# Attention and MLP on one core: the decoding buffers get a pool of their own, two weight sums move into the second token group, and the products get new orders

## The chip, the cores and the metric

One core of one Trainium2 chip runs the whole program. The metric is the device time of one launch in microseconds (us). Inputs lie in the device's memory at the start and the output must lie there at the end. Before the change three runs took 1042.72, 1043.13 and 1045.06 us; the median is 1043.13 us.

## The reference

Sigmoid attention (8 batches, 12 heads, 448 tokens, head size 64) feeds a two-layer MLP with a gated activation. The MLP weights arrive as 64-bit floats.

```python
scores = scale * np.matmul(q, k.transpose(0, 1, 3, 2)) - np.log(S)
attn = 1.0 / (1.0 + np.exp(-scores))
x = np.matmul(attn, v)            # then 3584 tokens x 768
h = x @ w_in                      # 768 x 2048
g = h * (1.0 / (1.0 + np.exp(-1.702 * h)))
out = g @ w_out                   # 2048 x 768
```

## The kernel before

**Stages.** The attention stage runs 48 pairs of heads, two pairs to a unit of 10.3 us, and stores its result by blocks of 512 tokens in device memory (tensor xd). Beside it the 16 pieces of the two weight matrices are decoded from 64-bit words (`decode`, L515): DVE and ACT build exponent and sign in buffers `raw64` and `e`, three DVE instructions build the number, and the result is kept on the chip (the 8 pieces of the first matrix) and stored in device memory (tensor f, one store of 768 KB for each of the 16 pieces).

**The MLP** is a fast matrix multiplication scheme: each of the two matrix products is done as 26 smaller products of sums of blocks. Tokens go in two groups: group 1 has 3 blocks of 512 tokens, group 2 has 4. Group 1 needs 20 of the 26 products of either layer, group 2 all 26, so 92 products in all. One product is 36 matmuls of 128x128 by 128x512 in fp32r (each operand is split in a rounded part and a rest, and three of the four cross terms are taken). For a product, DVE and ACT make the sum of weight blocks (`W_SUMS`: sums 8 to 25 are made from leaves 0 to 7), the sum of token blocks, a rounded copy (a cast, on ACT or DVE) and the rest (a subtraction on DVE) of both, and afterwards add the product into accumulators. In this text a product is named by its layer (0 or 1) and its number (0 to 25).

**Group 1 makes the weight sums**, splits them and saves the split pair in device memory (tensor c); group 2 fetches the saved pairs (`fetched`, L913). The six products that group 1 leaves out (numbers 3, 6, 8, 10, 12 and 17) have the sums 13, 25, 18 and 10 and the leaves 7 and 6. Their four sums are made in group 1 too and stored unsplit (`keep`, L847), and group 2 fetches them unsplit and splits them in place, as it does with leaves. All weight pairs go through a ring of two buffers (`wsplit`): a fetch for product n can only begin when product n-2 has ended. For layer 1, one half of the sums is made ahead during attention (`sums_ahead`, L855).

**SBUF.** All MLP operands lie in slots of an arena. Arena 0 (62 KB per partition) is there from the start; 48 KB of it are taken by the decoded pieces of the first matrix. Arena 1 (104 KB) and the second buffer of the `wsplit` ring lie in the memory of the attention pool `att`, which holds the decoding buffers too (`raw64` 24 KB, `e` 12 KB). They can be written when the last attention transfer has read its buffer.

**The order of the work** is made by a planner at build time (`Plan.run`, L113). It simulates PE, ACT, DVE, the SP queue and the DMA engines with estimated costs, and at each step emits the task that can begin first, ties going to the task whose product is earliest. `HORIZON` (L33) is how many PE tasks ahead of PE a slot may be taken; `KEEP`, `URGENT` and `SPARE` hold back room; `BACKLOG` and `PRESSING` hold back transfers while the modelled DMA backlog is over `BACKLOG` us, unless their product is within `PRESSING` tasks; `GIVE` says how long ACT may be busy for a cast to be still given to it; `RANKED` ranks the decoding among the attention pairs; `ISSUE`, `LANDING` and `PER_KB` are the modelled costs of a transfer. A layer 0 product is four PE tasks, a layer 1 product three. The last entry of each group in `GROUPS` is the order of its products. All transfers are issued by the SP queue, in the planned order.

## Time and profile before

| what | value |
|---|---|
| median of 3 runs | 1043.13 us |
| the profiled execution, its own time | 1042.31 us |
| its span, first to last instruction | 1040.2 us |
| mean granted TensorE clock | 0.993 |
| PE busy | 1012.3 us |
| DVE busy | 900.4 us |
| ACT busy | 631.4 us |
| DMA, both directions | 234.41 MB |

The time of a run is 2.1 us above the span of its profile; the profiled execution is 0.8 us below the median. The attention stage ends at 253.84 us on PE, and the 92 products follow.

### The profile page before, as it was taken

Reading aid. Unit: us, or ns where it says so; the run is one execution under the profiler, and the core shown is the slowest. Engines: PE = TensorE matmul, PEld = TensorE weight load, DVE = VectorE, ACT = ScalarE, POOL = GpSimd, SP = SyncE. Lnnn points to the kernel's source line nnn. Section 1 sums busy time; section 2 is a strip of 40 time slices with the busy share of each in tenths; the row PEclk is TensorE's granted clock in tenths of the full one; section 3 lists DMA queues with packets and bytes.
Section 4 is the critical chain, followed back from the end, with each engine's and each line's share of the span. In section 5 each row is a group of like instructions: output and inputs, shape, how many; then the busy total and the mean of one; then the engine's idle time right before and its main releaser. Section 6 shows DMA issues by size and latency. Waiting matters only on the chain.

```text
span 1040.2 us, 12860 instructions
## 1 busy us (share of the span) xinstructions
PE 1012.3 (97%) x5156; PEld 754.6 (73%) x5156; DVE 900.4 (87%) x628; ACT 631.4 (61%) x496; POOL 0.2 (0%) x4
## 2 busy tenths in 40 slices
PE   9999999999798999889999999999999999999998
PEld 5545454545686888778888777888888877888886
DVE  5999998994998988999989885786898989988876
ACT  6988998885466356676454424365676755553542
POOL 0000000000000000000000000000000000000000
PEclk9999999999899999999999999999999999999999
DMA  9999999996742544444565967544434534343487
GB/s 357 380 373 386 378 414 401 398 390 232 287 159 85 215 156 156 147 149 152 179 218 197 342 220 246 192 168 142 162 122 125 174 96 135 129 162 121 155 260 252
DMA packets 79402, 234.41 MB, mean 225 GB/s; under 512 B 7792, under 2 KB 17136, under 8 KB 77296
## 3 DMA queue, kind: packets, MB, share of 16 engines
q1 hardware_dynamic: 79344, 233.60, 62.6%
q8 instruction: 41, 0.67, 0.3%
q14 instruction: 17, 0.14, 0.0%
HBM read 148.64 MB, written 84.93 MB: 225 GB/s over the span
## 4 chain that ended last, share of the span: by engine, by line
PE 86%; DVE 5%; DMA 4%; issue 3%; ACT 3%; SPq 0%; ACTq 0%; DVEq 0%
PE p L810 62%; PE av L666 11%; PE sc L635 9%; PE av L679 2%; PE sc L651 2%; DMA w<-f 2%; DVE w L776 2%; DMA w<-c 2%; DVE arena L758 1%; DVE gp L979 1%; ACT w L773 1%; ACT arena L1150 0%; DVE arena L1184 0%; PE still L422 0%; ACT a L621 0%
## 5 line engine op out<-in xcount | busy, mean ns | idle before, releaser
L810 PE MATMUL p<-xp,w 128*128 128x512 f32 x1656 | 380.6, 392 | 11.9 <-issue 6.1
L810 PE MATMUL p<-gp,w 128*128 128x512 f32 x1656 | 379.9, 391 | 10.5 <-DVE w L776 2.7
L810 PEld LDWEIGHTS p<-xp,w 128*128 128x128 f32 x1656 | 312.5, 189 | 80.2 <-issue 11.3
L810 PEld LDWEIGHTS p<-gp,w 128*128 128x128 f32 x1656 | 311.3, 188 | 78.8 <-issue 7.8
L1150 ACT COPY arena<-p 128x2048 f32<-128x2048 f32 (+1 forms) x69 | 114.8, 1675 | 155.3 <-PE p L810 148.0
L621 ACT ACTIVATE a<-sc,bias 128x896 f32<-128x896 f32 x168 | 153.8, 1024 | 18.5 <-PE sc L635 18.5
L758 DVE TENSOR_TENSOR arena<-arena 128x1536 f32<-128x1536 f32 (+2 forms) x91 | 155.0, 1718 | 5.4 <-DMA xd<-x 5.0
L1184 DVE TENSOR_TENSOR arena<-arena,p 128x2048 f32<-128x2048 f32 (+1 forms) x60 | 120.5, 2027 | 22.6 <-PE p L810 17.5
L967 ACT CAST gp<-arena 128x2048 fp32r<-128x2048 f32 x42 | 80.3, 1912 | 63.9 <-PE p L810 48.2
L666 PE MATMUL av<-a,vraw 128*64 128x448 f32 x576 | 113.5, 543 | 0.0
L979 DVE TENSOR_TENSOR gp<-arena,gp 128x2048 fp32r<-128x2048 f32 x44 | 100.8, 2290 | 6.1 <-ACT gp L967 5.5
L635 PEld LDWEIGHTS sc<-qk 64*128 64x128 f32 x846 | 77.6, 184 | 23.1 <-issue 16.2
L635 PE MATMUL sc<-qk 64*128 64x448 f32 x846 | 92.2, 368 | 0.5 <-ACT a L621 0.5
L666 PEld LDWEIGHTS av<-a,vraw 128*64 128x64 f32 x576 | 39.2, 137 | 72.2 <-issue 46.9
L979 DVE TENSOR_TENSOR xp<-arena,xp 128x1536 fp32r<-128x1536 f32 x43 | 75.5, 1756 | 7.4 <-ACT xp L967 7.0
L773 ACT CAST w<-arena 128x768 fp32r<-128x768 f32 (+1 forms) x30 | 33.5, 1115 | 57.9 <-PE p L810 40.5
L758 DVE TENSOR_TENSOR arena<-arena,arena 128x1536 f32<-128x1536 f32 (+2 forms) x39 | 66.9, 1727 | 0.2
L776 DVE TENSOR_TENSOR w<-w 128x1536 fp32r<-128x1536 f32 (+1 forms) x30 | 47.9, 1597 | 20.2 <-ACT w L773 19.8
L967 ACT CAST xp<-arena 128x1536 fp32r<-128x1536 f32 x30 | 44.4, 1481 | 29.8 <-PE p L810 22.6
L776 DVE TENSOR_TENSOR w<-arena,w 128x1536 fp32r<-128x1536 f32 (+1 forms) x40 | 54.2, 1355 | 7.8 <-ACT w L773 7.4
L773 ACT CAST w<-w 128x1536 fp32r<-128x1536 f32 (+1 forms) x28 | 37.6, 1343 | 30.8 <-DMA w<-f 20.5
L503 DVE TENSOR_TENSOR qk<-qkraw,qk 128x896 fp32r<-128x896 f32 x47 | 50.7, 1090 | 1.6 <-ACT qk L497 0.9
(52 smaller groups left out, 514.1 us busy)
## 6 DMA issues: line engine op xcount, KB each, us to landing
w<-c SPq DMA_DIRECT2D x70, 768.0 KB, 5.5
c<-w SPq DMA_DIRECT2D x42, 768.0 KB, 5.0
w<-w SPq DMA_DIRECT2D x16, 1536.0 KB, 10.2
qkraw<-qk SPq DMA_DIRECT2D x47, 448.0 KB, 7.1
w<-f SPq DMA_DIRECT2D x38, 384.0 KB, 3.5
f<-arena SPq DMA_DIRECT2D x16, 768.0 KB, 8.2
vraw<-v SPq DMA_DIRECT2D x24, 448.0 KB, 7.9
c<-arena SPq DMA_DIRECT2D x14, 768.0 KB, 8.7
```

The lines of the kernel that those rows point to most:

```text
L503: lambda: nc.vector.tensor_tensor(lo(), src(), hi().bitcast(F32), op=ALU.subtract),
L621: nc.scalar.activation(a.tile, ps.tile[:, :, :S], AF.Sigmoid, bias=bias, scale=scale)
L635: nc.tensor.matmul(ps.tile[:, j, :S], lhsT=src[kk][rows, S + c * P : S + (c + 1) * P], rhs=src[qq][rows, :S], start=i == 0, stop=i == len( ...
L666: nc.tensor.matmul(ps.tile[cols, n % 2, :S], lhsT=vr.tile[:, at : at + D], rhs=a.tile[:, j], start=c == 0, stop=False, skip_group_check=True,)
L758: return task("DVE", cost, lambda: nc.vector.tensor_tensor(out(), x(), y(), op=op), deps, uses)
L773: t_hi = on_either((act(n), lambda: nc.scalar.copy(into()[:, 0], node.view())), (cast(n), lambda: nc.vector.tensor_copy(into()[:, 0], node ...
L776: t_lo = task("DVE", dve(n), lambda: nc.vector.tensor_tensor(into()[:, 1], node.view(), into()[:, 0].bitcast(F32), op=ALU.subtract), [t_hi ...
L810: nc.tensor.matmul(ps, lhsT=ws[:, a, c * P : (c + 1) * P], rhs=x[:, d, k], start=start and i == 0 and j == 0, stop=stop and i == len(todo) ...
L967: t_hi = on_either((act(n), lambda: nc.scalar.copy(part(0)(), node.view())), (cast(n), lambda: nc.vector.tensor_copy(part(0)(), node.view())),
L979: nc.vector.tensor_tensor(part(1)(), node.view(), part(0)().bitcast(F32), op=ALU.subtract)
L1150: t = on_either((act(self.n), lambda: nc.scalar.copy(view(), node.view())), (dve(self.n), lambda: nc.vector.tensor_copy(view(), node.view())),
L1184: nc.vector.tensor_tensor(view(), x.view(), y.view(), op=ALU.add if s0 == s else ALU.subtract)
```

## The change

It does these things:

- **Pools.** `raw64` and `e` leave the attention pool for a pool of their own on the left side of SBUF (`dec`), and the attention pool goes to the right side. Instead of one late pool there are two: the second `wsplit` buffer and a new arena 1 of 24 KB lie in the memory of `dec`, and arena 2 of 78 KB in that of `att`. There are two gates: the one of `dec` opens when the last users of the decoding buffers are planned, the other with the last users of the attention buffers. The ring `a` (sigmoid results) goes from 7 buffers to 6, and arena 0 from 62 to 64 KB.
- **Two weight sums.** Sums 25 (leaf 4 + sum 9) and 18 (leaf 3 + sum 11) are no longer made in group 1. Their parts, sums 9 and 11, are stored unsplit there as well, and group 2 loads both parts into two arena slots, adds them on DVE and splits the result into the ring buffer. This is once per layer for either sum.
- **Stores.** The decoded pieces 2 and 5 are no longer stored (14 stores instead of 16).
- **Shared pieces.** When a product's weight pair is still in the ring, it is used again instead of fetched and split again.
- **Orders.** Both groups get a new order of their products. Group 1 began with products 16, 15, 21, 23, 22, 5, 19, 25 of layer 0; now it begins with 22, 16, 5, 21, 19, 13, 7, 25. Its first layer 1 product is still the 20th. Group 2 began with 19, 4, 18, 14, 20, 22; now it begins with 13, 2, 16, 22, 15, 24. In group 2 the products 1 and 17, which both use leaf 6, now stand side by side in either layer. The last two products were layer 1 numbers 7 and 22; now they are 16 and 8.
- **Planner constants**, as in the diff.

```diff
-    qk=2, vraw=3, a=7, al=1, raw64=2, e=4, qkraw=5, x32=3,
+    qk=2, vraw=3, a=6, al=1, raw64=2, e=4, qkraw=5, x32=3,
...
-AREAS = 62, 104
-HORIZON, URGENT, SPARE, KEEP = 14, 4, 6, 16
+AREAS = 64, 24, 78
+HORIZON, URGENT, SPARE, KEEP = 11, 24, 6, 40
...
-BACKLOG, PRESSING = 6.0, 4
-GIVE = 1.5
-AHEAD = 14, 44
-RANKED = 6
...
-ATTENTION, LATE = ("qk", "vraw", "a", "al", "raw64", "e", "qkraw", "x32"), ("wsplit",)
...
+BACKLOG, PRESSING = 10.5, 42
+GIVE = 10.8
+AHEAD = 12, 46
+RANKED = 10
...
+ATTENTION, DECODING, LATE = ("qk", "vraw", "a", "al", "qkraw", "x32"), ("raw64", "e"), ("wsplit",)
...
-ISSUE, LANDING, PER_KB = 0.43, 2.2, 0.0027
+ISSUE, LANDING, PER_KB = 0.55, 2.8, 0.0026
...
-            if id(t) in gate:
-                gate.discard(id(t))
-                if not gate:
-                    area[1] = [end] * AREAS[1]
-                    room[0] += AREAS[1]
-                    found_at.clear()
+            for i, tasks in enumerate(gates, 1):
+                if id(t) in tasks:
+                    tasks.discard(id(t))
+                    if not tasks:
+                        area[i] = [end] * AREAS[i]
+                        room[0] += AREAS[i]
+                        found_at.clear()
...
+    for i, (name, tags) in enumerate((("dec", DECODING), ("att", ATTENTION))):
+        pool = first_stacks[i].enter_context(tc.tile_pool(name=name, bufs=2, side=SIDES[i]))
...
-        if True:
+        if n >= NW - NW // 4 or n in whole_pieces:
             stored[n] = dma(lambda: whole[n], f32, 2 * KB, [t_p], [f])
...
-    gate = plan.gate
+    gate = plan.gates[0]
...
         def fetched(m, r, b, into, first, halves):
             v, out, again = W_USES[r], [], []
+            if v >= LEAVES and v not in at_first:
+                s = plan.slot()
...
+                (u0, q0), *rest = made_of(v)
+                assert q0 == 1
+                ts = [load(u0, h, s, views[0]) for h in halves]
+                for u, q in rest:
+                    s1 = plan.slot()
+                    view = held(s1, f"wy{m}_{r}_{u}", N2)
+                    more = [load(u, h, s1, view) for h in halves]
+                    ts = [combine(dve(N2), views[0], views[0], view, q, [*ts, *more], [s, s1])]
+                return [split_piece(Node(s, views[0], ts), N2, into, b, first)]
...
+            key, ring = (m, W_USES[r]), plan.rings.get("wsplit", [])
+            if key in pieces_at and pieces_at[key][0][1] in ring[-BUFS["wsplit"] :]:
...
+        return [*out, *(v for v in range(LEAVES) if v not in out)]
```

## Rows read from the trace of the kernel before

**Rows 1.** Busy time of each engine in stretches of the span, counting only the matmuls of the products (line 810) and their weight loads: stretch, its length, PE busy (instructions), PEld busy, granted clock, DMA share, GB/s.

```profile
254.00:262.30 8.30, 8.29 (x36) 6.52 (x36) 1.00 0.56 186
262.30:268.40 6.10, 0.01 (x1) 0.04 (x1) 0.69 0.97 342
268.40:302.80 34.40, 34.40 (x145) 28.36 (x146) 0.96 0.51 187
302.80:322.50 19.70, 16.28 (x73) 13.19 (x71) 1.00 0.30 115
322.50:414.40 91.90, 91.90 (x398) 75.58 (x399) 0.98 0.46 172
414.40:480.00 65.60, 59.73 (x252) 47.82 (x251) 0.97 0.40 139
...
649.10:845.20 196.10, 196.09 (x864) 162.19 (x865) 1.00 0.45 149
```

**Rows 2.** Timeline of PE: start, length, what, how many; in brackets the idle time before the first of them and what ended it.

```profile
268.39 50.67 PE L810 MATMUL p<-xp,w 128*128 128x512 f32 x216 [6.10 <-issue]
322.49 99.98 PE L810 MATMUL p<-xp,w 128*128 128x512 f32 x432 [3.42 <-DVE xp L979]
422.31 8.32 PE L810 MATMUL p<-gp,w 128*128 128x512 f32 x36
432.72 0.47 PE L810 MATMUL p<-gp,w 128*128 128x512 f32 x1 [2.09 <-DVE arena L1184]
...
480.02 98.18 PE L810 MATMUL p<-gp,w 128*128 128x512 f32 x432 [0.50 <-DVE gp L979]
580.38 24.76 PE L810 MATMUL p<-gp,w 128*128 128x512 f32 x108 [2.18 <-DMA w<-c]
...
649.11 171.62 PE L810 MATMUL p<-xp,w 128*128 128x512 f32 x755 [0.85 <-DVE w L776]
```

**Rows 3.** Busy time of all engines in stretches: stretch, its length, PE (instructions), PEld, DVE, ACT, POOL, granted clock, DMA share, GB/s.

```profile
0.00:250.00 250.00, 248.46 (x1822) 129.85 (x1824) 221.09 (x240) 213.51 (x225) 0.20 (x4) 1.00 0.99 377
...
246.40:258.00 11.60, 11.60 (x70) 6.13 (x67) 2.73 (x3) 5.34 (x6) 0.00 (x0) 1.00 0.72 259
...
258.00:422.30 164.30, 154.78 (x667) 126.92 (x667) 149.57 (x88) 92.72 (x59) 0.00 (x0) 0.97 0.49 180
...
480.00:605.40 125.40, 122.97 (x541) 101.22 (x541) 110.40 (x75) 58.49 (x44) 0.00 (x0) 1.00 0.68 234
605.40:1036.30 430.90, 426.29 (x1872) 350.83 (x1872) 361.05 (x191) 223.95 (x138) 0.00 (x0) 1.00 0.50 165
```

**Rows 4.** Timeline of DVE and then of ACT around the end of attention, start and length first.

```profile
242.07 0.96 DVE L555 TENSOR_TENSOR expo<-expo,sign 128x1536 bf16<-128x1536 bf16 x1 [2.99 <-ACT sign L543]
...
244.66 1.75 DVE L562 SCALAR_TENSOR_TENSOR arena<-arena,expo 128x1536 f32<-128x1536 f32 x1
...
258.07 3.43 DVE L758 TENSOR_TENSOR arena<-arena 128x1536 f32<-128x1536 f32 x2 [5.04 <-DMA xd<-x]
261.53 3.43 DVE L758 TENSOR_TENSOR arena<-arena,arena 128x1536 f32<-128x1536 f32 x2
264.87 1.75 DVE L776 TENSOR_TENSOR w<-arena,w 128x1536 fp32r<-128x1536 f32 x1
266.54 1.75 DVE L979 TENSOR_TENSOR xp<-arena,xp 128x1536 fp32r<-128x1536 f32 x1
...
261.57 1.47 ACT L773 CAST w<-arena 128x1536 fp32r<-128x1536 f32 x1 [6.68 <-DMA arena<-xd]
```

**Rows 5.** Timeline of DVE between the two layers of group 1.

```profile
436.43 0.95 DVE L776 TENSOR_TENSOR w<-arena,w 128x768 fp32r<-128x768 f32 x1
437.29 2.29 DVE L758 TENSOR_TENSOR arena<-arena,arena 128x2048 f32<-128x2048 f32 x1
439.50 2.29 DVE L758 TENSOR_TENSOR arena<-arena 128x2048 f32<-128x2048 f32 x1
```

**Rows 6.** Groups of instructions of DVE from 254 to 480 us: busy time, mean ns of one, idle time before them.

```profile
L758 DVE TENSOR_TENSOR arena<-arena 128x1536 f32<-128x1536 f32 (+2 forms) x30 | 52.8, 1781 | 5.2 <-DMA xd<-x 5.0
...
L774 DVE CAST w<-arena 128x1536 fp32r<-128x1536 f32 (+1 forms) x7 | 6.3, 900 | 3.8 <-PE p L810 3.8
```

**Rows 7.** The chain of waits around one late weight piece: start, length, what.

```profile
639.91 0.34 SPq L471
640.29 5.40 DMA w<-f
645.79 1.49 ACT w L773
647.30 1.77 DVE w L776
649.11 196.12 PE p L810 x863
```

**Rows 8.** DMA issues of the whole span (line, count, KB each, median us from issue to landing).

```profile
w<-c SPq DMA_DIRECT2D x70, 768.0 KB, 5.5
...
w<-f SPq DMA_DIRECT2D x38, 384.0 KB, 3.5
```

**Rows 9.** The same view from 560 to 612 us alone, with its DMA queue (packets, MB, share of the 16 engines).

```profile
q1 hardware_dynamic: 4959, 16.12, 88.7%
...
w<-c SPq DMA_DIRECT2D x6, 768.0 KB, 6.0
```

More of the change, by code (lines that the diff above doesn't have):

```diff
@@ L85, in __init__ @@
     def __init__(self):
[L86 removed]
+        self.tasks, self.rings, self.early, self.slotted, self.gates = [], {}, [], [], ([], [])
     def buffer(self, tag):
@@ L505, in round_and_rest, with under, parts_of, made_of @@
         )
+    LEAVES, ops_of = NW // 2, {o[0]: o[1:] for o in W_SUMS[0]}
+    X_OF = [g[2][1] for g in GROUPS]
+    def under(vs):
+        seen, todo = set(), list(vs)
+        while todo:
+            v = todo.pop()
+            if v not in seen:
+                seen.add(v)
+                todo += ops_of.get(v, ())[:2]
+        return seen
+    W_USES = [v for v, _ in W_SUMS[1]]
+    at_first = under(v for r, v in enumerate(W_USES) if X_OF[0][r])
+    def parts_of(v):
+        if v < LEAVES:
+            return []
+        return [v] if v in at_first else [u for c in ops_of[v][:2] for u in parts_of(c)]
+    def made_of(v):
+        if v < LEAVES or v in at_first:
+            return [(v, 1)]
+        a, b, s = ops_of[v]
+        return [*made_of(a), *((u, s * q) for u, q in made_of(b))]
+    parts_later = {u for r, v in enumerate(W_USES) if v not in at_first for u in parts_of(v)}
+    whole_pieces = {n for r, v in enumerate(W_USES) for u, _ in made_of(v) if u < LEAVES for n in (u, LEAVES + u // 2)}
     KB = P * NW_EL * 4 / 1024
@@ L842, in sum_of @@
         sums.left[v] -= 1
-        return v, node, [t for u in set(sums.nodes) - had if u >= 8 for t in sums.nodes[u].done]
+        return node, [t for u, n in sums.nodes.items() if u not in had and u >= LEAVES for t in n.done]
     raw = {}
```

121 lines of the change are left out of this document (69 added, 52 removed).

## The prediction

> **What bounds the kernel now.** I read the busy times first. PE is busy for 97% of the span, and in the 250 us of attention it is never seen idle after its start [rows 3]; DMA is at a share of 0.99 there and DVE at 221 of 250 us. So the attention stage can only get worse, and what can be won lies in the 92 products behind it. Then the stretches with the products alone. In the undisturbed stretch from 649.1 to 845.2 us, 864 matmuls take 196.1 us, 0.227 us each; a product of 36 takes 8.17 us, and 92 take 751.7 us. They run from 253.8 to 1036.3 us, 782.4 us, so 30.7 us are lost. The rows give the places [rows 1]: 6.1 us without a matmul from 262.3, and 1.5 us behind it (145 matmuls in 34.4 us instead of 32.9, at a granted clock of 0.96, so partly at the lower of its two levels); 3.1 us from 302.8 to 322.5 (73 matmuls need 16.6 of 19.7 us) and 1.6 us behind it at a clock of 0.98; 8.4 us from 414.4 to 480.0 (252 need 57.2 of 65.6 us). From 480.0 to 605.4 it is 2.6 us (541 matmuls), and in the whole of group 2 6.0 us (1872 need 424.9 of 430.9 us) [rows 3]. Some 21 us are thus lost in the first 25 products, some 9 in the other 67.
>
> Then the timeline, for what ended each wait [rows 2]. In the first 25 it is DVE: a rest of a token piece, an accumulation, a token sum. From 258.0 to 422.3 DVE is busy 149.6 of 164.3 us [rows 3]: DVE paces PE there. It has a late start. In the last 11.6 us of attention it works 2.7 us [rows 3], because nothing has room: the decoding ends at 246.4 us (244.66 + 1.75), and the first sum for a product starts at 258.07, when the last transfer of attention has read its buffer; the second product's weight cast on ACT comes at 261.57, after the load into the new arena [rows 4]. In group 2 the waits are late weight pieces: 0.34 us of issue after the ring buffer is free, 5.4 of transfer, 1.49 of cast, 1.77 of subtraction, 9.0 together, against 8.17 us of the product that covers it [rows 7].
>
> **The change, part by part.**
>
> *The early arena.* The room of the decoding buffers (24 KB, four slots, and the second weight buffer) comes at 246.4 instead of some 258 us. That adds a wait of its own: the first user of this memory waits for the last decoding instructions, which wait for the sign on ACT [rows 4]. If this first user is a load, everything behind it on the SP queue waits too, the stores of the last attention results among it. At 246.4 us nothing is late through that. The new order helps: its first two products use leaves only, while the second product before the change needed a weight sum and a token sum. So in the new order DVE owes for the second product two weight rests and two token rests, 4 x 1.67 = 6.7 us; 1.67 us is the spacing of such instructions in a full stretch (264.87 to 266.54) [rows 4]. From 246.4 that is done at 253.1, before 262.0. The 7.6 us of the first gap go, with 1 us kept for a late load.
>
> *DVE through the first 25 products.* I counted from the tables, for both orders, what DVE must have done before a product can start: weight rests and sums, token rests and sums, accumulations of earlier products. With 1.67 us for 1536 elements, 2.20 for 2048 and 0.86 for 768 [rows 4, 5] this is, before and after, 28.9 and 27.2 us for product 4, 59.5 and 57.8 for product 8, 124 and 131 for product 17, 150 and 157 for product 20, 197 and 198.5 for product 26, 292 and 295 for product 40. Product 26 of the new order stands for 20 layer 0 and 6 layer 1 token rests and weight rests, 12 and 7 token sums, 16 and 5 weight sums, 19 and 3 accumulations. Before, product 26 started at 480.0 [rows 2], 222 us after DVE's start at 258: 1.128 times the work, since DVE also waits, does casts and works ahead. With the same factor the new order starts it at 247 + 198.5 x 1.128 = 470.9, a gain of 9.1 us; for product 20 (factor 1.094) it is 418.6 against 422.3, a gain of 3.7. If DVE waited for nothing, PE alone would set 458.2 for product 26, a gain of 21.8. The larger `GIVE` hands casts to ACT: the seven weight casts that DVE does here take 6.3 us [rows 6], and ACT is busy only 92.7 of 164.3 us [rows 3]. They cost nothing on ACT while it has that idle time, and DVE pays by waiting for them. I take half, 3 us. Bounds 3.7 and 21.8; I take 9.1 + 3, less 1 for the late load and 1 because the work for products 17 and 20 has grown by 7 us: 10 us, near the lower bound, since the row of the same engine in the same stretch is the nearest one.
>
> A rule of the Trainium skill speaks against the change here. By the Trainium skill, VectorE: DVE Perf Modes, section on the TRN2 errata, each DVE instruction pays a fixed latency that lies between instructions, and a two-input fp32 operation of N elements takes (N + 151)/0.96 ns; by that an estimate for 1536 elements is 1757 ns, and the mean in the rows is 1781 ns for that form with its rarer sizes [rows 6]. The rows show starts only 1.67 us apart, so neighbours overlap by 0.08 us, and the measurement decides. With that figure of the Trainium skill in the sum, the work before product 26 would be about 208 us instead of 198.5, and at the same factor the start 481.6 instead of 470.9.
>
> *The two weight sums.* Group 1 loses two DVE sums of layer 0 (2 x 1.67) and four halves of layer 1 (4 x 0.86), two of these in attention; that is in the counts above. Group 2 gets four sums of 1.67 us, 6.7 us, and loses two rests, 3.3 us, through the shared pieces. Over the whole program the new orders add six accumulations of 1536 elements (94 instead of 88), 10 us. In products 26 to 40 DVE's work grows from 101 to 105 us, in group 2 from 340 to 343. It is busy 110 of 125 us and 361 of 431 us there [rows 3], so some 15 and 70 idle us cover this; without cover it costs these 7 us.
>
> *Weight pieces in group 2.* Before, 24 of 52 products fetch an unsplit piece into the ring, the 9.0 us path. After, 18 do; four make their sum in slots that can be filled early, so that behind the free buffer only cast and rest are left (3.3 us), and two need no fetch. The losses at such products are 0.7 to 1.5 us, where the transfer took over 5 us; the usual 3.5 us for 384 KB is hidden [rows 8]. Five or six such losses in 24 make about 0.25 per piece; six fewer are worth 1.5 us. Against that stands the new beginning: second, third and fourth product all fetch unsplit pieces while the token blocks are loaded, where even saved pieces took 6.0 us instead of 5.5 [rows 8, 9]. If each of the three loses 1 us, it is 3 us. I take zero for both, bounds -2 and +6. The sixteen loads of 384 KB instead of eight, eight of them for parts, have half of the DMA time free [rows 3].
>
> *The rest, at nothing.* The ring of six sigmoid buffers: a unit writes six, and PE finishes all value matmuls of one unit before the next unit's first scores, so no sigmoid waits. Two stores of 768 KB less relieve a DMA that is full in attention. The new modelled costs are in the planner only, and act through the order. The looser `PRESSING` and `BACKLOG` do too: more transfers stand in the SP queue at once. In attention a reordered queue could delay the head pairs' loads; nothing in the trace prices that but the full DMA, so the bound there is 0 to 3 us, and I take 0. HORIZON at 11 tasks is still 2.75 products.
>
> **Sum.** The profiled execution had 1042.3 us, 2.1 above its span and 0.8 below the median. From the median: 1043.1 - 10 = 1033.
>
> **Rivals.**
>
> B, *DVE has no slack to use the head start with.* For: the work before product 20 grows by 7 us, more than half of the 11 us that DVE starts earlier, and accumulations are spread no better. Against: half of the idle time stood before 258 us. Then the gain is that of product 20, 3.7 us, or less; the time is 1039 to 1041, say 1039.5.
>
> C, *a backlog of transfers at the start of group 2.* From 560 to 612 us DMA is at 88.7% [rows 9] and the one saved piece that took too long cost PE 2.18 us [rows 2]. With transfers let through up to 42 tasks ahead and a backlog of 10.5 instead of 6 us, a ring fetch stands behind 4.5 us more. It decides once a fetch lands later than 8.2 us after its buffer is free: then each product of the loading time pays 2 to 3 us. Over the six or seven products in which the blocks of group 2 are loaded that is 14 to 17 us, and with the gain of 10 the time is 1047 to 1050. Against: in the rest of group 2 DMA is half idle, so the backlog ends.
>
> D, *the early arena comes late.* The decoding is ranked lower than before (`RANKED` 10) and its last sign waits for ACT as it is [rows 4]; if it ends with attention, room comes at 258 as before, and only the order is new. Then it is 1041 to 1045, say 1043.
>
> E, *nearly all of the first loss goes*: 20 us, 1023.
>
> **Chances.** Forecast (1027 to 1038) 0.55, B 0.17, C 0.12, D 0.11, E 0.05. The range from 1026 to 1044 leaves out C and E. Faster by over 0.2% (below 1041.0), about what a measurement can tell from no change, holds the forecast, B and E, 0.77; within 0.2% is D, nearly whole, 0.10; slower is C with the edge of D, 0.13.
>
> **What would show it.** Right: DVE works through the last 10 us of attention; no gap of several us after the first product; the 20th product starts before 418, the 26th near 468; the losses of group 2 stay near 6 us. Wrong: the first write into the new arena comes only at 255 or later (D); waits for DVE before products 3 to 8 as long as now (B); waits for weight transfers between 570 and 680 us (C); gaps in attention.

## The result: 1014.98 us, 18 us below the forecast

The changed kernel took 1014.98 us (median of 4 runs, 1013.42 to 1016.78), the kernel before 1043.22 in the same job: a ratio of 0.9727 (95%: 0.9702 to 0.9751). It is faster, as forecast, but by 28 us where the prediction said 10, and outside its range (1026 to 1044). The profiled execution of the changed kernel had 1016.45 us, its span is 1014.6; against the profiled execution of before the span is 25.6 us shorter, and 25.6 us is what the rows below can account for. The other 2.6 us are the spread of single executions around the medians.

PE, timeline of the changed kernel (start, length, what, count, idle time before it and what ended it), to be read beside [rows 2]:

```profile
254.91 155.98 PE L846 MATMUL p<-xp,w 128*128 128x512 f32 x684 [0.27 <-DVE xp L1047]
410.73 16.48 PE L846 MATMUL p<-gp,w 128*128 128x512 f32 x72
427.05 8.32 PE L846 MATMUL p<-xp,w 128*128 128x512 f32 x36
...
444.15 138.83 PE L846 MATMUL p<-gp,w 128*128 128x512 f32 x611 [0.39 <-DVE w L812]
582.82 24.89 PE L846 MATMUL p<-xp,w 128*128 128x512 f32 x109
608.84 188.79 PE L846 MATMUL p<-xp,w 128*128 128x512 f32 x827 [1.13 <-DVE w L812]
797.46 180.12 PE L846 MATMUL p<-gp,w 128*128 128x512 f32 x793
```

The first 19 products (684 matmuls) run without a break. The 20th starts at 410.73 us instead of 422.31. At 444.15 stands the second matmul of the 24th, so the 26th starts 71 matmuls later, at 444.15 + 71 x 0.227 = 460.3, instead of 480.02. All waits of PE in the products together:

```profile
PE p L846 <- DVE w L812: 2.0, 4, 1.1
...
PE p L846 <- DVE xp L1047: 0.3, 1, 0.3
```

That is 2.3 us, where [rows 2] alone has 6.10, 3.42, 2.09 and 2.18. Busy time of all engines in the stretches of [rows 3] (PE, PEld, DVE, ACT, POOL, granted clock, DMA share, GB/s):

```profile
246.40:258.00 11.60, 11.33 (x72) 5.90 (x69) 10.91 (x8) 7.94 (x8) 0.00 (x0) 1.00 0.78 281
258.00:422.30 164.30, 164.30 (x724) 135.23 (x723) 153.44 (x88) 107.93 (x70) 0.00 (x0) 1.00 0.50 187
```

DVE works 10.9 of the last 11.6 us of attention instead of 2.7, and 153.4 us instead of 149.6 in the stretch behind it, in which PE no longer waits at all. Four lines of DVE's timeline show the early start:

```profile
240.13 1.75 DVE L598 SCALAR_TENSOR_TENSOR arena<-arena,expo 128x1536 f32<-128x1536 f32 x1
...
245.39 1.75 DVE L812 TENSOR_TENSOR w<-arena,w 128x1536 fp32r<-128x1536 f32 x1
...
257.38 3.54 DVE L794 TENSOR_TENSOR arena<-arena 128x1536 f32<-128x1536 f32 x2
266.71 1.76 DVE L812 TENSOR_TENSOR w<-arena,w 128x1536 fp32r<-128x1536 f32 x1 [5.79 <-ACT w L809]
```

The last decode ends at 241.9 us, 4.5 us earlier than before, and DVE begins the work for the second product at 245.39 instead of 258.07 [rows 4].

**A measure for all runs.** A product takes 8.17 us on PE. From the start of the first product to the start of the 20th (19 products, 155.2 us) and from there to the end (73 products, 596.5 us), whatever is above these sums is lost. One profiled execution each:

| kernel | lost before the 20th product | lost from there on |
|---|---|---|
| before | 13.2 | 17.5 |
| after | 0.6 | 3.9 |
| thin7 / thin20 | 13.5 / 9.8 | 16.3 / 17.3 |
| pad4 / pad8 / pad_layer | 1.2 / 10.1 / 8.8 | 2.4 / 3.2 / 3.0 |
| cast7 | 4.0 | 2.0 |
| no_share / a_backlog | 0.5 / 0.5 | 5.5 / 2.4 |
| new_g2_alone | 13.6 | 17.1 |
| old_g1 | 12.3 | 63.0 |
| late_arena2 | 27.7 | 60.0 |
| give | 24.2 | 36.9 |
| old_constants | 17.9 | 13.7 |
| old_dma | 21.2 | 24.1 |
| a_swap / swap22 | 0.5 / 12.6 | 18.9 / 38.7 |

For before, the first is 422.31 - 253.84 - 155.2 (starts from [rows 1, 2]), the second 1036.3 - 422.3 - 596.5. So 12.6 us were won before the 20th product and 13.6 behind it, and 1.1 lost because the first product starts that much later. What a kernel loses ahead of its first product is not in the table: old_constants starts it at 260.47 us and old_dma at 258.15, 5.6 and 3.2 us later than the changed kernel. Of the 13.6, the six products at the change of layers (20th to 25th, 49.0 us of matmuls) gave 8.1: they took 57.7 us before and 49.6 after. The other 5.5 come from the 26th product to the end.

DVE's share in this is read from the same columns as above, from DVE's start to the 26th product and then for the six products alone, first in the kernel before, then in the changed one:

```profile
258.07:480.00 221.93, 206.54 (x883) 168.16 (x882) 205.12 (x122) 133.17 (x89) 0.00 (x0) 0.97 0.46 165
422.30:480.00 57.70, 51.83 (x217) 41.28 (x216) 55.56 (x35) 40.45 (x30) 0.00 (x0) 0.97 0.36 123
```

```profile
245.39:460.30 214.91, 214.25 (x968) 172.87 (x965) 200.93 (x117) 138.15 (x94) 0.00 (x0) 1.00 0.52 190
410.70:460.30 49.60, 49.21 (x217) 40.39 (x216) 46.77 (x29) 31.43 (x23) 0.00 (x0) 1.00 0.53 183
```

In the six products DVE had 55.6 us of work before, in 57.7 us, and waited 1.8 us. There its work paced PE. In the changed kernel it has 46.8 us in 49.6: 8.8 us less work stand beside the 8.1 us won.

### The profile page after: what moved, and what is told of

Same layout as the page of the kernel before. It is cut to its first block, busy times and chain, and to the rows that moved or that the text cites. A ratio compares the mean times of both kernels' runs of the same rounds, so it can differ in the third digit from the quotient of the medians.

```text
span 1014.6 us, 12887 instructions
## 1 busy us (share of the span) xinstructions
PE 1006.6 (99%) x5156; PEld 751.3 (74%) x5156; DVE 886.0 (87%) x614; ACT 642.2 (63%) x500; POOL 0.2 (0%) x4
## 4 chain that ended last, share of the span: by engine, by line
PE 95%; DMA 2%; ACT 1%; DVE 1%; issue 0%; SPq 0%; ACTq 0%; DVEq 0%
PE p L846 72%; PE av L702 11%; PE sc L671 9%; PE av L715 2%; PE sc L687 2%; DMA w<-f 2%; DVE w L812 1%; DMA qkraw<-qk 1%; ACT w L809 0%; ACT a L657 0%; SPq L475 0%; DVE xp L1047 0%; ACT xp L1035 0%; DVE qk L507 0%; DVE qk L502 0%
## 5 line engine op out<-in xcount | busy, mean ns | idle before, releaser
L1218 ACT COPY arena<-p 128x2048 f32<-128x2048 f32 (+1 forms) x66 | 110.1, 1673 | 128.2 <-PE p L846 121.0
L1252 DVE TENSOR_TENSOR arena<-arena,p 128x2048 f32<-128x2048 f32 (+1 forms) x59 | 119.3, 2040 | 20.6 <-PE p L846 14.4
L1035 ACT CAST gp<-arena 128x2048 fp32r<-128x2048 f32 x46 | 87.9, 1910 | 60.8 <-PE p L846 56.7
L794 DVE TENSOR_TENSOR arena<-arena,arena 128x1536 f32<-128x1536 f32 (+2 forms) x66 | 123.7, 1890 | 0.8 <-DMA arena<-xd 0.2
L1047 DVE TENSOR_TENSOR gp<-arena,gp 128x2048 fp32r<-128x2048 f32 x46 | 105.3, 2289 | 20.8 <-ACT gp L1035 20.4
L794 DVE TENSOR_TENSOR arena<-arena 128x768 f32<-128x768 f32 (+2 forms) x62 | 97.8, 1589 | 0.2
L671 PEld LDWEIGHTS sc<-qk 64*128 64x128 f32 x846 | 77.5, 184 | 23.9 <-issue 17.9
L809 ACT CAST w<-arena 128x1536 fp32r<-128x1536 f32 (+1 forms) x44 | 52.3, 1189 | 53.2 <-PE p L846 41.8
L1035 ACT CAST xp<-arena 128x1536 fp32r<-128x1536 f32 x42 | 62.1, 1482 | 27.4 <-PE p L846 17.1
L812 DVE TENSOR_TENSOR w<-arena,w 128x1536 fp32r<-128x1536 f32 (+1 forms) x44 | 61.2, 1390 | 13.7 <-ACT w L809 13.4
L1260 ACT ACTIVATE arena<-arena 128x2048 f32<-128x2048 f32 x26 | 49.4, 1915 | 6.2 <-DVE arena L1252 6.1
L809 ACT CAST w<-w 128x1536 fp32r<-128x1536 f32 (+1 forms) x24 | 31.7, 1322 | 25.9 <-DMA w<-f 21.2
## 6 DMA issues: line engine op xcount, KB each, us to landing
w<-w SPq DMA_DIRECT2D x16, 1536.0 KB, 10.1
```

Source lines behind the costliest of these rows:

```text
L671: nc.tensor.matmul(ps.tile[:, j, :S], lhsT=src[kk][rows, S + c * P : S + (c + 1) * P], rhs=src[qq][rows, :S], start=i == 0, stop=i == len( ...
L794: return task("DVE", cost, lambda: nc.vector.tensor_tensor(out(), x(), y(), op=op), deps, uses)
L809: t_hi = on_either((act(n), lambda: nc.scalar.copy(into()[:, 0], node.view())), (cast(n), lambda: nc.vector.tensor_copy(into()[:, 0], node ...
L812: t_lo = task("DVE", dve(n), lambda: nc.vector.tensor_tensor(into()[:, 1], node.view(), into()[:, 0].bitcast(F32), op=ALU.subtract), [t_hi ...
L1035: t_hi = on_either((act(n), lambda: nc.scalar.copy(part(0)(), node.view())), (cast(n), lambda: nc.vector.tensor_copy(part(0)(), node.view())),
L1047: nc.vector.tensor_tensor(part(1)(), node.view(), part(0)().bitcast(F32), op=ALU.subtract)
```

## The experiments

Two theories stood at the start: that DVE's head start and the early room carry the 28 us, or that the new orders and the planner's constants do. There are two kinds of runs. In some, the instructions of a kernel keep their order, and work is only added or taken away. In the others an order or a constant is changed and the planner makes a new order of everything. The second kind turned out to say less about one part, and more about the plan as a whole.

### Work added to or taken from DVE, order kept

**pad4 and pad8.** The changed kernel with 4 or 8 idle DVE instructions at some 258.7 us.

```diff
+            if e == "DVE" and not gates[0] and t.key > side_end:
+                self.after += 1
+                if self.after == 9:
+                    self.pad()
...
+        for _ in range(4):      # 8 in pad8
+            nc.vector.tensor_tensor(x, x, x, op=ALU.max)
...
```

> The changed kernel in its own order of instructions, with four extra DVE instructions of 1.67 us (6.7 us; the maximum of a tile with itself) at 258 us, between two of the sums for the third product. DVE stands idle for 5.8 us right behind them, so that a delay of 6.7 should reach the third product with its last 1 to 3 us. Theory H: 1016 to 1018 us. Theory O: 1015 us, hidden.

Measured: 1015.32 us, ratio 0.973, no difference from the changed kernel. The pad took 7.13 us on DVE.

> The same with eight extra instructions (13.4 us), about the whole head start. Theory H: the delay reaches PE nearly in full beyond the 5.8 us of idle time, and DVE stays late behind it: 1023 to 1030 us. Theory O: PE waits once for some us and the rest is absorbed: 1015 to 1019 us.

Measured: 1024.53 us, ratio 0.9817 (0.9799 to 0.9834), 9.5 us more than the changed kernel. DVE's timeline, then PE's, then stretches of the product matmuls alone (PE, PEld, granted clock):

```profile
258.68 14.30 DVE L1324 TENSOR_TENSOR arena<-arena 128x1536 f32<-128x1536 f32 x8
```

```profile
278.13 22.10 PE L850 MATMUL p<-xp,w 128*128 128x512 f32 x86 [6.99 <-DVE xp L1051]
```

```profile
262.00:271.00 9.00, 9.00 (x41) 7.24 (x39) 1.00 0.43 164
...
278.00:288.00 10.00, 9.87 (x33) 8.00 (x34) 0.74 0.52 202
```

The pad lasts 14.3 us, somewhat more than the 12.7 us by which DVE starts earlier. It is paid once, in one wait of 7.0 us and a stretch at a granted clock of 0.74 behind it (33 matmuls in the time of 44). The later waits of the kernel before do not come back: the loss behind the 20th product stays at 3.2 us. The first 7 us are free, as in pad4, most of them since DVE idles 5.79 us there anyway (the row at 266.71 above).

**pad_layer.** The same 4 instructions in front of DVE's 82nd instruction (`self.after == 82`), at 398.9 us, where the next thing that PE waits for is the 19th product.

> The changed kernel in its own order, with four idle DVE instructions (1.67 us each, 6.7 us) in front of one DVE instruction some 15 to 20 us before the change of layers. If DVE has spare time there (theory Q: what matters is which instruction stands in front of which): under 2 us, 1015 to 1017. If DVE is the pace there (W): 4 to 7 us, 1019 to 1022, in one wait near the first layer 1 products.

Measured: 1023.11 us, ratio 0.9801 (0.9763 to 0.9839), some 8 us more. DVE, PE, and the stretches of the product matmuls:

```profile
398.90 7.13 DVE L1324 TENSOR_TENSOR arena<-arena 128x1536 f32<-128x1536 f32 x4
```

```profile
407.84 10.64 PE L850 MATMUL p<-xp,w 128*128 128x512 f32 x36 [5.79 <-DVE xp L1051]
```

```profile
407.80:418.40 10.60, 10.56 (x37) 8.56 (x38) 0.78 0.00 0
418.40:434.70 16.30, 16.30 (x74) 13.49 (x73) 1.00 0.42 146
```

7.1 us of work cost 5.8 us of waiting and 2.2 us of slower matmuls behind it (37 of them in 10.6 us, at a granted clock of 0.78: 0.50, the lower of the two levels, in the first 4 us, and 1.00 in the last 4.6). So at 399 us DVE has 1.3 us to spare in the changed kernel, and no more. It is just fast enough there: PE does not wait for it, and hardly anything is left over.

**thin7 and thin20.** The kernel before, with the first 7 or 20 sums of 1536 elements behind attention cut to 96 columns; the rest of the sum is left out.

```diff
-        return task("DVE", cost, lambda: nc.vector.tensor_tensor(out(), x(), y(), op=op), deps, uses)
+        def emit():
+            a, b, c = out(), x(), y()
+            if plan.ended and plan.cut and a.shape[-1] == N2:
+                plan.cut -= 1
+                if out not in (x, y):
+                    nc.gpsimd.memset(a[:, 96:], 0.0)
+                a, b, c = a[:, :96], b[:, :96], c[:, :96]
+            nc.vector.tensor_tensor(a, b, c, op=op)
...
```

> The kernel before the change in its own order of instructions, but the first seven sums of 1536 elements that DVE makes after attention handle 96 elements only (the rest is left out, and set to zero by POOL where the slot is new), so that DVE is relieved of some 10 us at once, about what the early arena gives. Theory H (DVE's lead decides, and with it the later waits go too): the waits at 302 to 322 and 414 to 480 us go as well, 1022 to 1029 us, the 26th product by 466 us. Theory S (the sequence decides at the change of layers): only the first gap and part of the second go, 1031 to 1037 us, and the six products from 414 to 480 us still lose 6 to 9 us.

Measured: 1043.19 us, ratio 0.9994 (0.9981 to 1.0007): nothing, less than either theory expected.

> The same with the first twenty such sums, some 28 us of DVE's work between 258 and 340 us. Theory H: no wait for DVE before the 26th product, 1018 to 1024 us. Theory S: the products around the change of layers still lose 6 us or more, 1028 to 1034 us.

Measured: 1038.17 us, ratio 0.9948 (0.9933 to 0.9963): 5 us. From 258 to 418.5 us DVE is busy 119.9 us instead of 145.8, and PE gains 3.4 of these 26 us before the 20th product, and 0.3 behind it. Where the rest went stands in DVE's waits of thin20 from 258 to 418.5 us (engine, line and releaser; us in total, times, longest):

```profile
DVE w L786 <- ACT w L783: 12.5, 3, 7.0
DVE xp L989 <- ACT xp L977: 7.8, 6, 3.4
DVE w L784 <- PE p L820: 6.4, 5, 3.3
DVE arena L1194 <- ACT arena L1160: 4.7, 3, 2.9
DVE arena L766 <- DMA arena<-xd: 3.7, 1, 3.7
```

These five are 35 us; all waits of DVE in the kernel before, from its start at 258.07 us to its 20th product, are 14.4. ACT's timeline of thin20 shows why it is late with a cast:

```profile
277.66 1.87 ACT L1160 COPY arena<-p 128x2048 f32<-128x2048 f32 x1 [5.87 <-PE p L820]
279.43 1.48 ACT L783 CAST w<-arena 128x1536 fp32r<-128x1536 f32 x1
```

ACT idles 5.87 us in front of the copy and does the cast right behind it, in the planned order. The cast for a later product stands behind the copy of an earlier product out of PSUM, and that copy waits until PE has ended it. DVE needs the cast, so it can't get ahead, however little it has to do. In this order DVE is tied to PE up to the 20th product, and its own speed matters little there. Of the six products from the 20th on the runs say nothing of the kind: no sum was cut in that stretch, and DVE is busy for 55.5 of their 56.2 us in thin20 too. And the first gap of 6.1 us, which is 5.17 us in thin7, has another bound; DVE's timeline of thin7:

```profile
258.73 0.26 DVE L766 TENSOR_TENSOR arena<-arena,arena 128x96 f32<-128x96 f32 x1
262.94 0.26 DVE L766 TENSOR_TENSOR arena<-arena,arena 128x96 f32<-128x96 f32 x1 [3.95 <-DMA arena<-xd]
```

The second product's sum waits for a load into the late arena until 262.9, 0.3 us after the first product's end; ACT's copy of that product, the cast and the rest take it from there to 267.8. The memsets that thin7 adds on POOL (1.25 us each) are not the bound: the second product's weight cast, which waits for one of them, comes at 260.83 us, before the 261.57 of [rows 4]. So two things were late at the same time in the kernel before, the load into the late memory and DVE. In thin7 the load alone makes the gap; that DVE alone would make it too is only argued from pad8, which is in the new order.

**cast7.** The changed kernel in its order, with 7 of the first 14 weight casts on DVE instead of ACT.

```diff
-            t.emits[e]()
+            by = e
+            if t.weight and e == "ACT" and t.key > side_end:
+                self.casts += 1
+                if self.casts % 2 and self.casts <= 14:
+                    by = "DVE"
+            t.emits[by]()
...
```

> The changed kernel in its own order of instructions, but every second one of the first fourteen weight casts that the plan gives to ACT in the product stage is issued by DVE at the same place (seven casts of 0.96 us, as many as DVE did before the change from 254 to 480 us). Theory K (casts on ACT are a main part of the gain): 1020 us or more. Theories H and S: 1014 to 1018 us.

Measured: 1017.78 us, ratio 0.9749 (0.9732 to 0.9765), 2.8 us more, at the edge of what the spread of the changed kernel (1013.42 to 1016.78) lets one tell; in the profile the 20th product starts 3.5 us later.

### One part undone, planned anew

**late_arena.** The decoding buffers' memory is given to the planner only with that of attention.

```diff
+    plan.gates[0].extend(plan.gates[1])
```

> The changed kernel, but the planner gets the room of the decoding buffers only with that of the attention buffers, as before the change (some 12 us later). Orders, constants and sums are those of the change. Theory H (the head start of DVE before the end of attention is what removes the waits of the first 25 products): 1023 to 1032 us, with gaps of several us after the first product and DVE as the releaser. Theory O (the new orders and planner constants remove them, the head start is worth little): 1015 to 1019 us.

Measured: 1098.26 us, ratio 1.0521 (1.05 to 1.0542), far outside both ranges. The same kernel once more, read by its profile:

> The kernel of the late arena once more, for its profile. What is read is where the 20th and 26th products start on PE (before the change 422.3 and 480.0 us, after it 410.7 and about 460.5); the end of group 2 is not compared, since the planner packs a nearly full arena anew. Theory H (the head start): 418 to 424 and 468 to 480 us, a gap of 6 us or more before the second or third product. Theory S (the order of group 1 makes the gain, by what it asks of DVE and of the late room for the first products and at the change of layers): at most 415 and 465 us.

Measured: 1098.83 us. The 20th product starts at 436.95 us and the 26th at 487.9, later than either theory said. PE and ACT:

```profile
318.05 35.67 PE L846 MATMUL p<-xp,w 128*128 128x512 f32 x144 [9.49 <-ACT arena L1218]
360.68 76.01 PE L846 MATMUL p<-xp,w 128*128 128x512 f32 x324 [6.96 <-ACT arena L1218]
...
768.95 19.15 PE L846 MATMUL p<-xp,w 128*128 128x512 f32 x72 [8.95 <-DVE arena L1252]
...
1009.66 83.78 PE L846 MATMUL p<-gp,w 128*128 128x512 f32 x360 [14.24 <-ACT p L1138]
```

```profile
316.13 1.87 ACT L1218 COPY arena<-p 128x2048 f32<-128x2048 f32 x1 [1.82 <-DVE xp L1047]
```

The gap behind the first product is not there: the new plan runs two products through. What comes is another kind of wait. The copy of a finished product into the arena starts at 316.13, when a rest of a token sum has been made (DVE, 314.33 to 316.09) and its slot is free; PE waits for the copy, because the copied product holds its PSUM buffer. It is room that is missing, and DVE, which works without a break from 303.66 to 316.09 us, is late in giving it back. And 60 us are lost behind the 20th product, most of them in group 2, where both plans have the same memory.

**old_g1.** The changed kernel with the group 1 order of the kernel before (the first entry of `GROUPS`).

> The changed kernel with the order of group 1 that stood before the change; early arena, constants, sums and the order of group 2 stay. Theory H: the gain is mostly kept, 1015 to 1021 us (DVE owes 6.7 us more for the second product). Theory O: most of the loss of the first 25 products is back, 1026 to 1034 us.

Measured: 1088.58 us, ratio 1.0436 (1.0419 to 1.0453), more than either theory said. PE:

```profile
272.81 150.61 PE L846 MATMUL p<-xp,w 128*128 128x512 f32 x648 [8.71 <-DVE xp L1047]
423.26 8.32 PE L846 MATMUL p<-gp,w 128*128 128x512 f32 x36
433.68 0.47 PE L846 MATMUL p<-gp,w 128*128 128x512 f32 x1 [2.09 <-DVE arena L1252]
...
463.20 16.80 PE L846 MATMUL p<-gp,w 128*128 128x512 f32 x73 [1.70 <-DVE gp L1047]
480.31 122.47 PE L846 MATMUL p<-gp,w 128*128 128x512 f32 x539 [0.31 <-DVE w L812]
...
998.90 83.84 PE L846 MATMUL p<-gp,w 128*128 128x512 f32 x360 [14.24 <-ACT p L1138]
```

With the early arena and all else of the change, the old order has the first gap, starts the 20th product at 423.26 (422.31 in [rows 2]) and the 26th at 479.6 (480.02), with waits like those of [rows 2] between these two. So in this plan next to nothing is won of the 21 us and more that were lost before the 26th product.

The cause of its first gap is not what the old order asks of DVE. DVE starts early here too, at 247.24 us, and then stands idle for 12.1 us. DVE's row, and the DMA issues from 249 to 270 us (KB each, median us from issue to landing):

```profile
267.66 1.76 DVE L794 TENSOR_TENSOR arena<-arena 128x1536 f32<-128x1536 f32 x1 [12.13 <-DMA xd<-x]
```

```profile
k<-arena SPq DMA_DIRECT2D x4, 384.0 KB, 10.1
...
xd<-x SPq DMA_DIRECT2D x1, 448.0 KB, 11.6
```

The last transfer of attention took 11.6 us to land instead of 3.0 before and after the change, with six stores of weight sums issued in the 7 us ahead of it, and so the late memory came free at 267.5 us instead of 258. Behind this gap and the slow matmuls after it nothing more is lost up to the 20th product: the waits at 322 us of [rows 2] are gone in the old order as well. The plan of old_g1 also leaves out one wait: a sum is made in place over the decoded leaf 4 before that piece is stored, so that layer 1 number 25 multiplies half of its weights wrongly. Its 3312 matmuls are all there, and its time is taken as that of the same work.

The new order without the early arena could not be tried on the kernel before: its planner finds no place for all slots.

**a_swap and swap22.** One pair of products exchanged at the change of layers, in the changed kernel and, the other way, in the kernel before.

```diff
-(1, 25), (0, 14), (0, 6), (1, 15), (1, 19)      # a_swap
+(1, 25), (1, 15), (0, 14), (0, 6), (1, 19)
-(0, 12), (1, 15), (0, 7), (1, 6), (1, 16)       # swap22
+(0, 12), (0, 7), (1, 15), (1, 6), (1, 16)
```

> The changed kernel with its 22nd and 23rd product exchanged the other way (layer 1 number 15 ahead of layer 0 number 14); the plan is made anew. Q: the waits at the change of layers come back, 3 to 6 us in all, 1018 to 1021. W: DVE has the same work, no more than 1 us, 1015 to 1016. R: single waits of 5 us or more elsewhere, 1025 or more.

Measured: 1031.43 us, ratio 0.9881 (0.9842 to 0.992). Between the 20th and the 26th product 2.7 us come back, less than Q's 3 to 6; the rest is R, an 8.95 us wait in group 2.

> The kernel before, with its 22nd and 23rd product exchanged (layer 0 number 7 now stands ahead of layer 1 number 15), as the changed kernel has its last layer 0 product; the plan is made anew. Theory Q (each wait at the change of layers belongs to the order of the products: three layer 1 products in a row need sums of layer 0's results that are made only then): the waits of 2.1 to 2.4 us at the 21st and 22nd product go, the 26th product starts 3 to 6 us earlier, 1037 to 1040 us. Rival W (DVE has too much work there, in whatever order): the waits move to other products, their sum stays near 8 us, 1042 to 1044. Rival R (a new plan runs out of slots somewhere else, as in other runs): one or two waits of 5 us or more at other places, 1045 or more.

Measured: 1062.06 us, ratio 1.0179 (1.014 to 1.0217). The 2.09 us stayed, the 2.36 us went, and a wait of 7.66 us for a rest came at the 24th product, so that the 20th to the 25th took 61.4 us instead of 57.7; then a 10 us wait in group 2. Q falls for this pair: this exchange does not explain the change of layers. DVE is busy for 57.8 of these 61.4 us.

**new_g2_alone.** The kernel before with the new order of group 2 (the second entry of `GROUPS`).

> The kernel before the change with the new order of group 2 alone. If that order made the 4 to 5 us that were won behind the 26th product: 1037 to 1040 us. If they came from the weight pieces (sums in slots, shared pieces, planner): 1042 to 1045 us.

Measured: 1044.21 us, ratio 1.0011 (0.9996 to 1.0025): nothing.

**no_share.** Shared pieces off (`if False and key in pieces_at ...`).

> The changed kernel, but the second product with leaf 6 of either layer in group 2 fetches and splits its weight piece again; the planner plans anew. Theory W (fewer pieces on the long fetch path make the gain of group 2): 1016 to 1020 us with the first 26 products unchanged. If the plan runs out of arena slots, as three others did, single waits of some 9 us for the copy of a product show in group 2 and the run tells nothing about W.

Measured: 1016.47 us, ratio 0.974 (0.9725 to 0.9754): 1.5 us, at the edge of what can be told.

**The constants.** First all but HORIZON and the modelled costs, then GIVE alone, then the hold on transfers alone, then the modelled costs of a transfer alone (with that of a matmul, 0.2267 us for 0.227).

```diff
-HORIZON, URGENT, SPARE, KEEP = 11, 24, 6, 40     # old_constants: all these lines
+HORIZON, URGENT, SPARE, KEEP = 11, 4, 6, 16
-BACKLOG, PRESSING = 10.5, 42                     # a_backlog: this one
+BACKLOG, PRESSING = 6.0, 4
-GIVE = 10.8                                      # give: this one
+GIVE = 1.5
-AHEAD = 12, 46
+AHEAD = 14, 44
-RANKED = 10
+RANKED = 6
-ISSUE, LANDING, PER_KB = 0.55, 2.8, 0.0026       # old_dma, alone
+ISSUE, LANDING, PER_KB = 0.43, 2.2, 0.0027
```

> The changed kernel with the planner constants of before (BACKLOG, PRESSING, GIVE, AHEAD, RANKED, URGENT, KEEP; HORIZON stays at 11, as the planner finds no place for all slots at 14). Pools, orders, sums and modelled landings are those of the change. Theory K (the constants, casts on ACT above all, took the waits away): the waits of the first 25 products come back, the 20th product starts at 418 us or later, 1025 us or more. Theory S: the 20th product starts by 413 us, 1015 to 1020 us.

Measured: 1049.92 us, ratio 1.0069 (1.0045 to 1.0093), 35 us more than the changed kernel. The 20th product starts at 433.60 us, as theory K had it; 5.6 us of this stand ahead of the first product.

> The changed kernel with GIVE at 1.5 as before the change: casts go to DVE again when ACT is busy for longer. Theory K: DVE gets some 10 to 20 us of casts in the product stage and falls behind, 1022 to 1035 us. Theory S: 1014 to 1018 us.

Measured: 1071.01 us, ratio 1.0275 (1.0257 to 1.0294), far above theory K as well. Its three longest waits, 8.5 to 9.9 us, are for a copy, an addition and a write-back of finished products, as in late_arena2, and not for casts.

> The changed kernel with BACKLOG 6 and PRESSING 4 as before, a new plan of it. Theory H (holding transfers back makes weight pieces of group 2 late, so that the looser constants are where the losses behind the 20th product went from 17.5 to 3.9 us): the waits of PE for weight pieces come back in group 2, 5 to 9 us, 1020 to 1025. Rival N (nothing): 1014 to 1017. Rival R (a plan that runs out of slots, waits of 5 us or more for copies and additions): 1030 or more.

Measured: 1014.88 us, ratio 0.9733 (0.9712 to 0.9753): nothing, as rival N had it.

> The changed kernel with the planner's modelled costs of a transfer as before (issue 0.43, landing 2.2, 0.0027 us per KB; and its cost of a matmul, 0.2267 for 0.227); nothing else of the program changes but the plan that comes of it. Theory P (the measured costs matter because loads for the first products and weight pieces of group 2 were planned too late by the old ones): waits for DMA or for casts behind a load, 1 to 3 us each, 3 to 10 us in all, 1018 to 1025. Rival N (as forecast, nothing): 1014 to 1017. Rival R (a plan that runs out of slots: copies and additions of finished products that wait for a slot, 5 us or more each): 1030 or more.

Measured: 1058.95 us, ratio 1.0145 (1.0116 to 1.0174), as rival R had it. PE, and the chain behind its wait at 766 us on DVE and ACT:

```profile
316.80 18.41 PE L846 MATMUL p<-xp,w 128*128 128x512 f32 x72 [9.39 <-ACT arena L1218]
...
766.00 68.69 PE L846 MATMUL p<-xp,w 128*128 128x512 f32 x288 [8.95 <-DVE arena L1252]
```

```profile
757.08 4.48 DVE L1252 TENSOR_TENSOR arena<-arena,p 128x2048 f32<-128x2048 f32 x2 [0.64 <-PE p L846]
...
763.56 2.29 DVE L1252 TENSOR_TENSOR arena<-p,arena 128x2048 f32<-128x2048 f32 x1 [0.32 <-ACT p L1138]
```

```profile
761.66 1.87 ACT L1138 COPY p<-arena 128x2048 f32<-128x2048 f32 x1 [3.10 <-DVE arena L1252]
```

The wait of 8.95 us, which old_g1, late_arena2, give and a_swap have too, is a chain with nothing beside it: two additions of a finished product (4.5 us), then ACT writes an accumulator back into PSUM so that PE can add to it (1.9), then one more addition (2.3), then PE. The products of old_dma have 24 such write-backs, those of the changed kernel 24 too, and there PE waits for none of them.

**leaf2_h11.** The kernel before, with a second product that needs leaves only.

```diff
-[(0, 3), (0, 16), (0, 6), (0, 15), ..., (0, 23), (0, 22), (0, 5),
+[(0, 3), (0, 16), (0, 22), (0, 6), (0, 15), ..., (0, 23), (0, 5),
-HORIZON, URGENT, SPARE, KEEP = 14, 4, 6, 16
+HORIZON, URGENT, SPARE, KEEP = 11, 4, 6, 16
```

> The kernel before with layer 0 number 22, which needs leaves only, as its second product; HORIZON is 11 instead of 14, since with 14 the planner finds no place for all slots. Only the first gap (6.1 us before the second product) is read, since the plan behind it is a new one. Theory L (the second product waits for a load into memory that comes free with the end of attention): the gap is 3.5 us or more. Theory S (it waits for its weight sum and token sum on DVE): it falls to 2.5 us or less.

Measured: 1097.28 us, ratio 1.0517 (1.0479 to 1.0555). PE, then SP:

```profile
274.35 8.02 PE L810 MATMUL p<-xp,w 128*128 128x512 f32 x28 [11.54 <-DVE xp L979]
```

```profile
263.80 0.37 SPq L471 DMA_DIRECT2D xd<-x  x1
266.63 2.19 SPq L471 DMA_DIRECT2D arena<-xd  x4
```

Here even the first product waits 11.5 us for the late memory: attention itself ends later, its last transfer is issued at 263.8 us instead of 254.9, and the loads at 266.6, when it has read its buffer. By the letter theory S came true, since no gap stands before the second product; but the wait has only moved ahead of the first. So the run decides nothing between the two.

## Why the prediction was right in sign and short in size

**Right: the head start.** The signs named for it are there: DVE busy in the last 10 us, no gap after the first product, the 20th before 418. Only the 26th came 8 us earlier than the named 468. That pad8 costs 9.5 us, near the 9.1 that the forecast took for product 26, is no proof of the size: 7 of its 14.3 us are hidden, 2.4 are slow matmuls, and the order is one that the forecast did not reckon with. **Right: the casts on ACT**, in kind: 3 us were taken, cast7 costs some 3. **Right: the loose hold on transfers** costs and gives nothing (a_backlog), so rival C does not occur. Rivals B and D do not either: DVE used its head start, and the last decode, after which there is room, ended at 241.9 us, earlier still than the 246.4 that was assumed. The shared pieces are worth 1.5 us, and from the 26th product on 5.5 us less are lost (556.2 us became 550.8), within the bounds of -2 to +6 but at their upper end, where zero was taken; PE's waits there fell from 7.5 us to 1.6, nearly all of them for weight pieces.

**The step that failed** is the factor: "1.128 times the work, since DVE also waits, does casts and works ahead. With the same factor the new order starts it at 247 + 198.5 x 1.128 = 470.9". It carried the waits and the casts of the old order over to the new one, in proportion to DVE's work. In the changed kernel the factor is (460.3 - 245.4) / 198.5 = 1.083, for product 20 (410.7 - 245.4) / 157 = 1.053 instead of 1.094. That is 9 to 10 us of the missing 18; 5.5 lie behind the 26th product, and 2.6 the spread between profiled executions and medians.

The two long stretches in the section on the result show what the factor hid. The 26th product starts 19.7 us earlier. DVE starts 12.7 us earlier, of which a copy of attention and the first product's rest, which before stood ahead of 258.07, take 2.9: 9.8 us are left, where the forecast had 9.1. DVE's other work is 7.0 us less, 6.3 of it the weight casts [rows 6], where the forecast had 3. Its waits fall from 16.8 to 14.0 us, where the forecast kept them. And the 2 us taken off for a late load and for the work of products 17 and 20 did not come. This is bookkeeping along DVE, and no run takes the four apart.

For product 20 the counts themselves spoke against the factor. Before the change DVE owed 150 us for product 20 and started at 258: 408 us. PE alone needs 253.8 + 155.2 = 409. So DVE had in sum enough time, and the 13.2 us lost there were not its work. thin20 shows it: 26 us of work less, and only 3.4 us come out of it. What kept the waits in thin20 was the order of the queues, where casts stand behind copies that wait for PE. For the six products behind it the counts say the opposite: DVE had 55.6 us of work there for 49.0 us of matmuls, and the new order has 46.8; that this is the cause is a reading, since no run takes work away there. old_g1 shows that the early arena alone does not bring the gain, though its first gap has a cause of its own, the late transfer. The stated reason for staying "near the lower bound", that "the row of the same engine in the same stretch is the nearest one", took a property of a plan for one of an engine. Rival E, which had all of this loss go, was given 0.05.

**The rule that spoke against the change.** By the Trainium skill, VectorE: DVE Perf Modes, section on the TRN2 errata, an estimate for the work before product 26 was 208 us, and its start at the same factor 481.6. The trace agrees with it for the length of one instruction (1.75 us in [rows 4]). It doesn't agree for the spacing of neighbours that don't depend on each other, which stand 1.67 us apart (from 264.87 to 266.54 in [rows 4]; in the changed kernel from 266.71 to 268.39). By that figure of the Trainium skill, as an estimate, the 157 us before product 20 would be 165, and with the 9.6 us that DVE waits in the changed kernel between 258 and 410.7 us the product would start at some 420 instead of 410.7. For instructions that each need the one before, the last section has a spacing of 1.79.

**What the parts are worth can't be added up.** Undone alone and planned anew, they cost 83 us (late_arena), 74 (old_g1), 56 (give), 44 (old_dma), 1.5 (no_share) and 0 (a_backlog): together many times the 28 us. Each of the four large ones pushed the plan into waits for slots or for write-backs which neither kernel has. So these runs show that the early room and the new order are each needed for this plan. They don't show that either is worth that much. At fixed order, pad8 prices a DVE that is 14.3 us later at 9.5 us, and cast7 seven casts at some 3.

**What stays open.** Which feature of the new order removes the 8.1 us at the change of layers: DVE has 8.8 us less to do there, but which of the sums and additions have moved, and whether that is enough, was not tried, and one pair of products gives back 2.7 in one direction and wins nothing in the other. And where the 5.5 us behind the 26th product come from, beyond the 1.5 of the shared pieces: not from the order of group 2 alone, nor from the hold on transfers. The casts were not tried there: from 480 us on DVE made 17.6 us of them before, and makes none from 460 us on in the changed kernel.

## What to carry to other kernels

When an engine paces another, count its work and compare it with the time of the engine that waits, stretch by stretch, before calling it too slow. Here the sums fitted up to the 20th product, where the waits lay in the order of the queues and their room, and did not fit in the six products behind it. A test at fixed order, adding or removing idle instructions at one place, prices a cause; a new plan prices a plan. Added and removed work need not be alike: 7.1 us added cost nothing at one place (pad4) and 8 us at another (pad_layer), and 26 us removed gave back 5 (thin20).

## What the runs showed of the hardware

Instructions of DVE that each read what the one before has written start further apart: 8 in place (the maximum of a tile with itself) took 14.3 us (pad8) and 4 took 7.13 (pad_layer), 1.79 us each from start to start, where independent neighbours of the same size start 1.67 us apart [rows 4].

The two waits of PE that the pads made cost more than their length. Behind 5.8 us the next 37 matmuls took 10.6 us instead of 8.4 at a granted clock of 0.78 (pad_layer), behind 7.0 us some 10 us went by at 0.74 (pad8); before the stop the clock was 1.00 in either. So 2.2 and 2.4 us were lost on top of these waits.
